# Softmax sums and V products on 32-column tiles of the matmul array, and a new order of all steps, in a sliding-window attention and gMLP kernel

## The chip, the cores and the metric

The kernel runs on one core of one Trainium2 chip. Its time is the device time in microseconds (us) of one execution. The engines are PE (TensorE: matmul), ACT (ScalarE), DVE (VectorE), POOL (GpSimd) and SP (SyncE, which issues nearly all DMAs). Matmuls write to PSUM, which holds eight banks of 128 partitions by 512 f32.

## The reference

The inputs are q, k and v of shape [8, 8, 576, 64] (batch, head, position, head dimension) in f32, and the weights of a gMLP block. Per batch:

```
scores = (q @ k.T) / 8, kept where 0 <= t - s < 64, else -1e9
attn   = exp(scores - max); attn /= sum(attn) + 1e-9
x      = (attn @ v) with the heads side by side        # [576, 512]
h      = relu(x @ w_in)                                # [576, 1024]
u, v   = h[:, :512], h[:, 512:]
v_n    = (v - mean(v)) / sqrt(var(v) + 1e-6)           # over the 512
v_s    = w_spatial @ v_n + b_spatial                   # over positions
out    = (u * v_s) @ w_out                             # [576, 512]
```

## The kernel before

The program is a list of named steps. Each step belongs to an engine and has inputs and buffers that it must wait for. A long text, ORDER, gives the order in which steps are issued, with the engine of each and the number of the buffer or PSUM bank that it takes. Each engine works through its own steps in that order, and semaphores make it wait for the steps of other engines. So the order around any step is written out by hand, with no scheduler behind it. In a name such as `P4_10` the first digit is the batch, the next the half g of the heads (four heads each), and the last a part. `_r` stands for the remainder (the last 64 positions), `_0` to `_4` in the gMLP steps for blocks of 128 rows, the fifth being 64 wide.

Attention, per batch and half:

- `ldq`, `ldk`, `ldv` are loads, issued by SP in order, into buffers `nat` (eight, also used for the weights) and `natv` (four). `cq`, `ck`, `cv` cast to f16, `tq`, `tk` transpose q and k on DVE, and `sl`, `su`, `s4` make a copy of v shifted by 64 positions. POOL, ACT and DVE share the casts and copies.
- `S` (line 490, remainder 557): the scores, transposed, in products of 32 rows of the array by 128 columns, four side by side, 64 positions wide. Their result fills two pairs of banks.
- `E` (L497, on ACT) takes the exponential of two heads at a time into `e2`; `M` (L500, on DVE) takes the minimum with a mask, which zeroes what lies outside the window.
- `Z` (L513, remainder 580): the softmax sums, as a product with ones. Two matmuls of 64 columns side by side, one for each of two heads, put each head's sums on 64 partitions. There are two Z steps per half, one for each pair of heads, u = 0 and 1.
- `N` and `n` (L539, L541, both on ACT): logarithm of the sums, then exp of its negative, which is the reciprocal.
- `P` (L524, remainder 593): the product with v, for each 64 positions and two heads, two matmuls of 64 columns side by side. `X` (L532, 601; DVE) multiplies it with the reciprocal and leaves x transposed, two heads (128 rows of x) per tile.

The gMLP block, per batch:

- `V` (value half of x @ w_in), then `Vr` (relu, ACT, L658), `Vb` and `Va` (statistics, DVE, L660, L662), `L1` and `L2` (ACT, L705, L707), `A` (normalize into `vn`, DVE, L717). `V_4` (L691, L694) pairs the last 64 rows of one batch with the last output rows of the batch before and always uses two tiles of 64 columns.
- `U` (the other half) and `Ur` (relu, ACT, L746); `G` (the spatial product) and `Ge` (times u, DVE, L776); `O` (the product with w_out), `Oe` (copy to `ob`, ACT, L635) and `st` (store, SP).

`V`, `U`, `G` and `O` go through the helper `halves`. It issues each product either whole (128 x 128, L608) or as two halves of 64 columns side by side (L611). A rule, `halved`, picks the halved ones from ORDER: those that stand between Z or P steps, which use 64 columns too. `D` steps (L816) are products of zeros that fill time before real work is ready; there are 27, and their place is in ORDER.

Weights are loaded in pieces (`ldwin`, `ldwsp`, `ldwo`) and cast (`cwin`, `cwsp`, `cwo`). `ldwin100` to `ldwin111` bring the value half of w_in, `ldwin000` to `ldwin011` the other. `W` transposes w_spatial on PE and `We` copies it out of PSUM.

## Time and profile before

| | |
|---|---|
| median of 3 runs | 199.65 us (199.64 to 199.70) |
| span of the profiled execution | 198.2 us |
| mean granted PE clock | 0.998 |
| matmuls, all instructions | 3337, 7839 |
| DMA traffic, mean rate | 42.74 MB, 216 GB/s |
| L513 (Z), 64 matmuls of 64 columns by 512 | 386 ns each, overlapping |
| L524 (P), 512 matmuls of 64 columns by 64 | 196 ns each, overlapping |
| L497 (E), 32 on ACT | 1024 ns |
| L316 (casts of q and k), 10 on ACT | 1156 ns |
| L319 (the same on POOL), three pieces each | 530 and 559 ns a piece |
| L431 (transposes), 32 on DVE | 1246 and 1240 ns |

The profiled execution's span stands 1.4 us below the median of the runs: a run's time also holds what lies around the first and last instruction. The busy time of an engine is the union of its instructions; matmuls overlap in the array, so the time that a PE step costs is read from the starts of successive steps in the timeline, not from the duration of one matmul. The idle time shown for an engine counts only where that engine is the one that others wait for.

### The profile page before, as it was taken

How to read it: one execution, taken by the hardware profiler on the slowest of the kernel's cores; microseconds unless marked ns; L12 is line 12 of the kernel's file. 1: busy time of each engine (PE TensorE's matmuls, PEld its weight loads, DVE VectorE, ACT ScalarE, POOL GpSimd, SP SyncE). 2: the span in 40 equal slices, each digit the busy share in tenths (PEclk: the TensorE clock that was granted, in tenths of full speed). 3: DMA queues.
4: the chain of work that ended last, by engine and by line, in shares of the span. 5: the costliest groups of instructions: out<-in, count | busy, mean ns of one | idle time of the engine just before them, and what ended most of it. 6: DMA issues, size and time to landing. Idle time of an engine off the chain costs nothing.

```text
span 198.2 us, 7839 instructions
## 1 busy us (share of the span) xinstructions
PE 187.3 (94%) x3337; PEld 109.7 (55%) x3337; DVE 158.4 (80%) x306; ACT 168.4 (85%) x305; POOL 76.9 (39%) x147
## 2 busy tenths in 40 slices
PE   7788999999999999989999999999999999999991
PEld 2333565666556665565476567466465565764450
DVE  4799999999796899869999798887958684757420
ACT  2589889878899999989999999999999999558341
POOL 5232584747776689121999299100000000000000
PEclk9999999999999999999999999999999999999999
DMA  6998999999689989989999993878721110500535
GB/s 221 384 289 178 383 365 222 308 366 372 140 203 286 343 239 255 276 195 266 322 253 235 262 294 83 251 205 228 235 107 65 49 41 5 215 0 0 179 115 187
DMA packets 50278, 42.74 MB, mean 216 GB/s; under 512 B 39361, under 2 KB 39489, under 8 KB 50242
## 3 DMA queue, kind: packets, MB, share of 16 engines
q1 hardware_dynamic: 50018, 41.91, 71.9%
q8 instruction: 26, 0.43, 0.9%
q10 hardware_dynamic: 224, 0.33, 0.5%
q14 instruction: 10, 0.08, 0.1%
HBM read 32.79 MB, written 9.44 MB: 213 GB/s over the span
## 4 chain that ended last, share of the span: by engine, by line
PE 42%; ACT 20%; DMA 20%; DVE 6%; SPq 5%; issue 3%; POOL 3%; POOLq 0%
PE bank L611 17%; PE bank L608 17%; DMA nv<-in_v_dram 9%; DMA nk<-in_k_dram 7%; SPq L445 4%; DMA ws<-in_moe_w_spatial_dram 4%; ACT e L497 3%; ACT ob L635 3%; ACT lz L539 3%; ACT hs L316 2%; ACT lz L541 2%; PE pair L490 2%; PE bank L524 2%; ACT ru L746 2%; ACT vs L658 2%
## 5 line engine op out<-in xcount | busy, mean ns | idle before, releaser
L497 ACT ACTIVATE e<-pair 128x1024 f16<-128x1024 f32 x32 | 31.8, 1024 | 2.8 <-PE pair L490 2.6
L611 PE MATMUL bank<-wspT,vn 128*64 128x512 f16 (+3 forms) x440 | 32.4, 296 | 0.3
L776 DVE TENSOR_TENSOR g<-bank,ru 128x512 f16<-128x512 f32 (+1 forms) x40 | 24.6, 629 | 9.1 <-PE bank L608 4.4
L660 DVE BATCH_NORM_STATS2 st<-vs 128x6 f32<-128x512 f16 (+1 forms) x40 | 25.7, 671 | 2.8 <-ACT vs L658 2.8
L658 ACT ACTIVATE vs<-bank 128x512 f16<-128x512 f32 (+1 forms) x40 | 23.0, 602 | 5.6 <-PE bank L611 3.2
L532 DVE TENSOR_TENSOR x<-bank,lz 128x512 f16<-128x512 f32 x32 | 21.4, 683 | 6.5 <-PE bank L524 5.0
L746 ACT ACTIVATE ru<-bank 128x512 f32<-128x512 f32 (+1 forms) x40 | 21.6, 562 | 4.5 <-PE bank L608 4.4
L635 ACT COPY ob<-bank 128x512 f32<-128x512 f32 (+1 forms) x39 | 22.8, 589 | 2.1 <-PE bank L608 1.9
L611 PEld LDWEIGHTS <-vn 128*64 128x64 f16 (+1 forms) x440 | 18.6, 110 | 10.7 <-issue 1.3
L319 POOL CAST hk<-nk 128x384 f16<-128x384 f32 x33 | 16.3, 530 | 19.3 <-DMA nk<-in_k_dram 18.9
L500 DVE TENSOR_TENSOR e<-e,mask 128x1024 f16<-128x1024 f16 x32 | 21.9, 701 | 1.2 <-ACT e L497 1.2
L611 PE MATMUL bank<-win,x 128*64 128x512 f16 x184 | 22.4, 379 | 0.0
L431 DVE STREAM_TRANSPOSE qT<-hq 128x576 f32<-128x576 f32 x16 | 19.8, 1240 | 3.2 <-POOL hq L319 3.0
L611 PE MATMUL bank<-x,win 128*64 128x512 f16 (+1 forms) x288 | 22.3, 298 | 0.0
L431 DVE STREAM_TRANSPOSE kT<-hk 128x576 f32<-128x576 f32 x16 | 19.9, 1246 | 0.7 <-POOL hk L319 0.4
L541 ACT ACTIVATE lz<-lz 128x512 f32<-128x512 f32 x32 | 19.7, 635 | 0.1
L539 ACT ACTIVATE lz<-bank 128x512 f32<-128x512 f32 x32 | 18.6, 606 | 1.2 <-PE bank L513 1.1
L717 DVE TENSOR_SCALAR vn<-vs,mv,ln 128x512 f16<-128x512 f16 (+1 forms) x40 | 15.8, 447 | 4.2 <-ACT ln L707 4.1
L319 POOL CAST hq<-nq 128x384 f16<-128x384 f32 x30 | 15.7, 559 | 7.4 <-DMA nq<-in_q_dram 6.4
L322 POOL COPY hs<-hv 64x512 f16<-64x512 f16 (+1 forms) x28 | 16.2, 607 | 4.4 <-issue 3.7
L816 PE MATMUL bank<-scratch 128*128 128x512 f16 (+1 forms) x68 | 15.6, 379 | 1.3 <-DVE scratch L257 1.3
L611 PE MATMUL bank<-wout,g 128*64 128x512 f16 x128 | 16.1, 380 | 0.0
(89 smaller groups left out, 333.0 us busy)
## 6 DMA issues: line engine op xcount, KB each, us to landing
nq<-in_q_dram SPq DMA_DIRECT2D x16, 576.0 KB, 6.0
nk<-in_k_dram SPq DMA_DIRECT2D x16, 576.0 KB, 5.8
nv<-in_v_dram SPq DMA_DIRECT2D x64, 128.0 KB, 5.2
out_dram<-ob SPq DMA_DIRECT2D x14, 512.0 KB, 4.7
wi<-in_moe_w_in_dram SPq DMA_DIRECT2D x8, 256.0 KB, 6.0
ws<-in_moe_w_spatial_dram SPq DMA_DIRECT2D x4, 288.0 KB, 7.0
nv<-in_v_dram SPq DMA_DIRECT2D x16, 64.0 KB, 4.8
wo<-in_moe_w_out_dram SPq DMA_DIRECT2D x4, 256.0 KB, 8.1
```

Source lines behind the costliest of these rows:

```text
L319: nc.gpsimd.tensor_copy(o[:, n:n + 384], i[:, n:n + 384])
L431: d = add(f"t{name}{b}_{g}", ("DVE", 1.09), key, lambda e: nc.vector.transpose(qt.t[:, :].rearrange("p (i j) -> p j i", j=18), h.t[:, :].b ...
L497: ex = add(f"E{b}_{g}{u}", ("ACT", 0.91), key, lambda e, u=u: nc.scalar.activation(e2[u].t[:, :, :], sc[u].t[:, :, :], AF.Exp, bias=0.0, s ...
L539: a = add(f"N{tag}", ("ACT", 0.06 + 0.00083 * n), key, lambda e: nc.scalar.activation(lz.t[:, 0:n], zb.t[:, 0:n], AF.Ln), deps=[z], acq=[l ...
L541: c = add(f"n{tag}", ("ACT", 0.09 + 0.00083 * n), key, lambda e: nc.scalar.activation(lz.t[:, 0:n], lz.t[:, 0:n], AF.Exp, bias=0.0, scale= ...
L608: nc.tensor.matmul(o[:, :], w, x, start=start, stop=stop)
L611: nc.tensor.matmul(o[c:c + 64, :], w[:, c:c + 64], x, start=start, stop=stop)
L635: lambda e: (nc.vector.tensor_copy if last else nc.scalar.copy)(view(), m.t[rows, 0:n]),
L658: rl = add(f"Vr{b}_{j}", ("ACT", 0.49), key, lambda e: nc.scalar.activation(vs.t[0:jn, :], m.t[0:jn, :], AF.Relu), deps=[pv], acq=[vs], us ...
L660: s1 = add(f"Vb{b}_{j}", ("DVE", 0.6), key + 0.02, lambda e: nc.vector.bn_stats(st6.t[0:jn, 0:6], vs.t[0:jn, :]), deps=[rl], acq=[st6], us ...
L746: lambda e, m=m, ru=ru, n=n: nc.scalar.activation(ru.t[:, 0:n], m.t[:, 0:n], AF.Relu), deps=[pu], acq=[ru], uses=[m])))
L776: lambda e, m=m, g=g, ru=ru, n=n: nc.vector.tensor_tensor(g.t[:, 0:n], m.t[:, 0:n], ru.t[:, 0:n], ALU.mult),
```

## The change

Three things change in the products, and ORDER is new from the first word to the last.

Z becomes one step per half: four matmuls of 32 columns, side by side, one for each head, so each head's sums stand on 32 partitions. There is one N and one n per half in place of two. P keeps two steps per half, but each now covers all four heads and every second head dimension: f = 0 the even, f = 1 the odd ones. It is made of 32-column matmuls, 32 in a step in place of 16, and reads v with a stride of 2. So a tile of x holds the even or the odd dimensions of four heads, and the rows of w_in are loaded in that order (even rows in one tile, odd rows in the other, 2 KB per row as before). The remainder's Z, N and n are 128 wide in place of 256, and `X_r` reads the reciprocal twice by a broadcast.

```diff
-        for u in (0, 1):
...
-                    for w in (0, 1):
-                        nc.tensor.matmul(zb.t[64 * w:64 * w + 64, :], ones[:, :], e2[u].t[:, w, :],
-                                         start=True, stop=True)
...
+                for hh in range(4):
+                    nc.tensor.matmul(zb.t[32 * hh:32 * hh + 32, :], ones[:, 0:32],
+                                     e2[hh // 2].t[:, hh % 2, :], start=True, stop=True)
+        z = add(f"Z{b}_{g}", ("PE", 0.22), key + 0.03, emit_Z, deps=mins, acq=[zb], uses=e2, mode="q")
...
-                        for w in (0, 1):
-                            nc.tensor.matmul(ob.t[64 * w:64 * w + 64, 64 * c:64 * c + 64],
-                                             vv[:, c // 2, 2 * u + w, :],
-                                             e2[u].t[:, w, 64 * c:64 * c + 64],
+                        for hh in range(4):
+                            nc.tensor.matmul(ob.t[32 * hh:32 * hh + 32, 64 * c:64 * c + 64],
+                                             vv[:, c // 2, hh, f:64:2],
+                                             e2[hh // 2].t[:, hh % 2, 64 * c:64 * c + 64],
                                              start=True, stop=True)
```

The gMLP products are whole or in four quarters of 32 columns; none is halved any more. Which are in quarters is written in ORDER (engine `PQ` in place of `PE`): 74 steps.

```diff
-HALVED = halved(2) | {f"U0_{i}" for i in range(5)}
+QUARTERED = {w.split(":")[0] for w in ORDER.split() if w.split(":")[1] == "PQ"}
...
     def halves(name, o, w, x, start, stop):
-        if name not in HALVED:
-            nc.tensor.matmul(o[:, :], w, x, start=start, stop=stop)
-            return
-        for c in (0, 64):
-            nc.tensor.matmul(o[c:c + 64, :], w[:, c:c + 64], x, start=start, stop=stop)
+        n = 32 if name in QUARTERED else 128
+        for c in range(0, 128, n):
+            nc.tensor.matmul(o[c:c + n, :], w[:, c:c + n], x, start=start, stop=stop)
```

```diff
-                                 st.t[:, 512 * f:512 * f + 512], moe_w_in[256 * g + 128 * f:256 * g + 128 * f + 128, cs]),
+                                 st.t[:, 512 * f:512 * f + 512],
+                                 moe_w_in[256 * g:256 * g + 256, cs].rearrange(
+                                     "(p f) n -> f p n", f=2)[f]),
```

The new order also hands casts and copies to other engines:

| step | before | after |
|---|---|---|
| cq | POOL 10, ACT 5, DVE 1 | POOL 11, ACT 4, DVE 1 |
| ck | POOL 11, ACT 5 | POOL 11, ACT 3, DVE 2 |
| cv | POOL 12, DVE 5, ACT 3 | POOL 16, ACT 3, DVE 1 |
| sl | ACT 10, POOL 7, DVE 3 | POOL 11, DVE 6, ACT 3 |
| su | POOL 13, DVE 4, ACT 3 | POOL 14, DVE 4, ACT 2 |
| s4 | POOL 8, ACT 7, DVE 1 | POOL 12, ACT 4 |

Four places of the new ORDER that matter below, cut from it. The first is the start of SP's loads, with the casts and PE steps between:

```diff
+ldq1_0:DQ:6 ... ldk1_1:DQ:7 ... ldq1_1:DQ:0 ... ldwin100:DQ:1 ... ldv1_10:DQ:2 ... ldwin101:DQ
...
+X1_00:DVE:3 ... tk2_0:DVE:3 S2_0:PE:0:1
+X1_01:DVE X1_11:DVE V1_1:PE:2
...
+s45_1:POOL ... ldv7_10:DQ:2 ... ldq6_0:DQ:1 ... cq6_0:POOL:3 ... sl5_00:POOL:3 ... s45_0:POOL ... ck7_0:POOL:0 ... su5_00:POOL
+P5_00:PE:3
...
+O7_2:PE:1 Oe7_2:ACT:1 st7_2:DQ
+U7_4:PE:0 O7_3:PE:2 Ur7_4:ACT:2 Ge7_4:DVE:9 O7_4:PE:1
```

Of the fillers, 23 now stand ahead of `V0_2`; `D12` stands just before `U0_1`, and `D11`, `D18` and `D8` stand in batches 1, 4 and 7.

## The prediction

> **What bounds the kernel now.** I read the page's busy shares first, then the stretches, the PE groups by shape, and the timeline.

> ```profile
> PE 187.3 (94%) x3337; PEld 109.7 (55%) x3337; DVE 158.4 (80%) x306; ACT 168.4 (85%) x305; POOL 76.9 (39%) x147
> ```

> ```profile
> core 0: us, PE busy (x) PEld busy (x) DVE busy (x) ACT busy (x) POOL busy (x), PEclk, DMA share, GB/s
> ...
> 45.00:70.00 25.00, 24.52 (x512) 15.72 (x496) 21.97 (x41) 23.52 (x44) 17.24 (x32) 1.00 0.94 268
> 70.00:95.00 25.00, 23.87 (x517) 14.28 (x513) 22.68 (x44) 23.68 (x43) 12.71 (x25) 1.00 0.93 246
> 95.00:120.00 25.00, 25.00 (x482) 14.96 (x482) 23.64 (x40) 24.27 (x47) 20.40 (x39) 1.00 0.93 267
> 120.00:145.00 25.00, 24.93 (x395) 14.27 (x392) 20.70 (x44) 24.81 (x47) 4.57 (x10) 1.00 0.67 194
> 145.00:170.00 25.00, 24.92 (x495) 15.05 (x493) 17.36 (x34) 24.68 (x45) 0.00 (x0) 1.00 0.17 58
> ```

> PE is full and ACT is nearly as full: 23.5 to 24.8 of every 25 us. DVE is close behind until 120 us. So there are two near-limits, PE and ACT, and a third, DVE, in the first 120 us. The chain of waits agrees, and two groups of ACT show what the change takes from it:

> ```profile
> PE 42%; ACT 20%; DMA 20%; DVE 6%; SPq 5%; issue 3%; POOL 3%; POOLq 0%
> ```

> ```profile
> L541 ACT ACTIVATE lz<-lz 128x512 f32<-128x512 f32 x32 | 19.7, 635 | 0.1
> ...
> L539 ACT ACTIVATE lz<-bank 128x512 f32<-128x512 f32 x32 | 18.6, 606 | 1.2 <-PE bank L513 1.1
> ```

> The numbers behind the bar are the group's busy us, then the mean ns of one. PE leads the chain, ACT and the loads share the rest.

> A busy PE is not a PE at its peak, so I price its work by start times in the timeline:

> ```profile
> 101.73 0.41 PE L513 MATMUL bank<-e,ones 128*64 128x512 f16 x2
> 101.95 0.25 PE L524 MATMUL bank<-e,hv 128*64 128x64 f16 x4
> ...
> 103.06 0.30 PE L580 MATMUL bank<-er,ones 128*64 128x128 f16 x4
> 103.17 1.05 PE L611 MATMUL bank<-wout,g 128*64 128x512 f16 x8
> 104.04 0.25 PE L524 MATMUL bank<-e,hv 128*64 128x64 f16 x4
> ```

> ```profile
> 143.75 1.25 PE L608 MATMUL bank<-wspT,vn 128*128 128x512 f16 x5
> 144.84 0.63 PE L608 MATMUL bank<-x,win 128*128 128x64 f16 x16
> 145.40 0.68 PE L490 MATMUL pair<-qT,kT 32*128 32x64 f16 x64
> 146.01 0.30 PE L580 MATMUL bank<-er,ones 128*64 128x128 f16 x4
> ```

> Five full products take 144.84 - 143.75 = 1.09 us, 217 ns each (216 by finer starts). Eight half ones take 104.04 - 103.17 = 0.87 us: a pair, two 64-column matmuls side by side, costs the same 217 ns. A Z step (one pair) takes 0.22 us, Z_r (two pairs of 128) 0.11 us. Sixteen P matmuls take 0.25 us by their starts: 15.6 ns each, 31 ns per pair. S runs four matmuls on 32 rows each side by side: 64 take 0.61 us, 7.8 ns each or 31 ns per four, plus a gap. That gap is the price of changing shape: the first start after a full product of another shape comes 312 ns after the last one, not 216, so 96 ns, and the same for every change of shape in the trace.

> **Where PE loses time.** I sum PE's steps in listed order at these prices, fillers (D) left out: 166 us stand ahead of the last product, O7_4, which starts at 193.46. So 27.4 us are lost ahead of it: 20.3 by 30.2 us (U0_2, 9.9 us of work done: loads and start-up), 25.4 by 88.6 us, 27.4 at the end. What the change can win beyond PE's own work is in the 7 us after the start-up, 5 of them between 30 and 89 us.

> **The change, part by part.**

> *Z.* Sixteen (batch, half) groups had two Z steps of one pair each and get one step of four quarter matmuls. If a quarter pack (four matmuls of 32 columns) costs the 216 ns that a full product and a pair cost, 16 x 0.216 = 3.46 us go; Z_r saves one 55 ns pack in eight batches, 0.44. All of it is on PE.

> *P.* Twice the matmuls, half the columns: 288 packs before and after. At 31 ns per pack, the S row for four side by side, the cost is 0. At 15.6 ns per matmul, the P row, a pack is 62 ns. I take 31: S shows matmuls, each with its own weight load, starting 7.8 ns apart. The stride of 2 in the weights is also in S's kT reads.

> *74 gMLP steps in quarters.* 297 packs of 512 and 92 of 64; before, 356 and 164 were pairs. At 216 and 31 ns the cost is 0; fewer 64-wide packs in pieces saves 0.15. The trace has no product with four full-height streams. Lower bound 0, because one and two streams both take 216. Upper bound two pairs in a row, 432 ns: 313 packs (with Z) x 0.216 = 68 us. I take 0, since neither one to two streams nor S's four tiles cost anything, and keep 1 ns per pack = 0.31 us for the range. Weight loads become four per pack; one of 64 columns shows 110 ns, one of 128 shows 98, and they run beside the 216 ns of the pack ahead (PEld is 55% busy).

> *Shape changes.* Counting both listings: 48 become 63 between real steps, because V_4 stays in pairs and more products run whole: +15 x 0.096 = +1.44 us.

> PE's own work: -3.46 - 0.44 - 0.15 + 1.44 = **-2.6 us**.

> *ACT.* Sixteen N (606 ns) and sixteen n (635 ns) go: -19.9 us. The remainder's pair shrinks from 256 to 128 elements, by the slope of these rows 8 x 0.215 = -1.7. Casts and copies move to POOL (two ck, one cq, seven sl, three s4 and others): about -10. ACT falls from 168 to some 137 us, POOL rises to about 90, DVE stays at 158 (its X and M count is unchanged; X_r reads its factor broadcast, 421 ns before and between that and the 683 of a 512-wide X now: 0 to 2.1 us over eight, DVE's idle 40 us cover it). ACT stops being a limit. But PE lost only 2 us after 89 us although ACT was 97 to 99% busy there; the 5 us before that come with DVE at 88 to 95% too. I give back 2.4 of the 7 us.

> *Start-up.* In SP's queue the last value half of w_in now stands behind all eight q/k loads of two batches and one piece of batch 1's v. By bytes, 1.28 MB more lie ahead of it, 3.4 us at the page's best 384 GB/s; but SP stood blocked twice in the old order (v issues of 3.19 and 2.47 us), which may shrink. For the u half (before U0) it is 0.77 MB, 2.0 us. V0_1 needs that half; it started at 23.6 with 4.5 us of work done and now has 4.0 ahead of it. Bounds 0 to 2 us; I take 0.8, as V0_1 to V0_2 cover 5.5 us of waiting for the u half. Batch 2's loads are wanted earlier (S2_0 after 15.5 us of work, was 23.0): tk2_0 stands ahead of X1_01 and X1_11 on DVE, and V1_1 waits for these: +0.8. Four fillers (0.43 each) stand later, after D12; a filler in a gap costs nothing, else +1.3 for three; D25 and D26 (1.0) go from the same phase. Net 0.

> *SP's queue later.* ldq6_0 now stands behind ldv7_10, which waits until s45_1 on POOL frees its buffer; that place is 1.2 us of PE work ahead of cq6_0, where it was 7.7. Behind cq6_0 on POOL stand sl5_00, s45_0, ck7_0 and su5_00, for which P5_00 waits. POOL's buffers are free long before, so it can run ahead: 0 to 3.4 us, I take 0.2. Stores ahead of a reused ob buffer can issue 4 us or more before; nothing.

> *Tail.* U7_4 moves behind O7_2, so Ur7_4 (0.38) and Ge7_4 (0.42) with their hand-overs, about 1.05 us, lie beside O7_3 alone (0.86): +0.2.

> Sum: -2.6 - 2.4 + 0.8 + 0.8 + 0.2 + 0.2 = -3.0, and some of the reordering's waits may share one gap, -0.2. So -3.2 on a span of 198.2 (the median lies 1.4 above it): **196.4 us**.

> **Rivals.**

> *The floor is per matmul.* If a column-tiled matmul cannot start sooner than P's 15.6 ns, the 380 packs of 64 (288 + 92) take 62 instead of 31 ns: +11.8 us, **208.2**. For it: the P row itself. Against it: S at 7.8 ns. It decides from 39 ns a pack (380 x 8.4 ns = 3.2 us). [...]

> *Four streams are slower than two.* From 10 ns a pack (313 x 10 ns) the gain is gone; at 288 ns, as if only three ran at once, +22.5 us, **219**. For it: no row shows four. Against: two cost nothing. [...] The trace shows the two of a Z pair starting 4 ns apart, yet the next pair 216 ns after the first, so the offset is not added.

> *DVE takes the place of ACT.* Between 60 and 84 us of PE work the new listing gives DVE 28.5 us of row durations (27.5 with their overlap) against 24.0 of PE. If DVE arrives there without a lead, +3.5: **199.9**, no gain. For it: DVE's 22 to 23.6 of 25 us now. Against: the stretch ahead gives it 9.9 for 12. It decides when more than 3 us are lost there.

> *ACT was the cause of nearly all waits.* Then 4.5 more than PE's work goes: **192.5**.

> **How the numbers follow.** Forecast 0.58; ACT the cause 0.08; waits come back on DVE or in SP's queue 0.17, of which 0.07 within 0.2% (0.4 us, about what a measurement of this kernel can tell from no change) and 0.10 slower; streams slower by 10 ns or more 0.10; floor per matmul 0.07. Faster 0.66, same 0.07, slower 0.27. The range runs from 192.5, the ACT case, to 201.0, which takes in the returned waits and the slow start-up (2.0 for 0.8, 3.4 for 0.2 in SP's queue) and leaves out the floor, most of the streams case and half of the ACT case, 0.2. The forecast's own range is 193.2 to 199.

> **What would show it.** Right: Z steps of 0.22 us from start to start, P steps of 0.25, quarter products 0.86 (V, U, O) and 1.08 (G); ACT near 137 us, POOL near 90; V0_1 near 24.5 us, about 164 us of PE work and some 26.5 us lost ahead of O7_4. Wrong: a P step of 0.5 us (floor); quarter products above 0.90 (streams); PE waiting for DVE tiles x or vn between 80 and 110 us; SP issuing q loads of batch 6 less than 6 us before S6_0.

## The result, and the profile after

The changed kernel takes **223.1 us** (220.7 to 226.6, four runs) against 199.6 for the kernel before, measured beside it: a ratio of 1.115, 95% interval 1.108 to 1.123. The prediction said 196.4, range 192.5 to 201.0, and put 0.27 on slower. It was wrong in sign and outside its range. Its slowest rival, four streams at 219 us, comes near in time, but the traces show another mechanism. Medians count all runs; ratios and intervals, here and below, leave out runs over 1.5% above the fastest of their kernel, among them one of a_vlong at 307.8 us with a granted clock of 0.56.

The profiled execution took 220.7 us with a span of 218.9. From its page (busy shares, then the granted clock and DMA share in 40 slices, then the queue that brings instructions, then the chain of waits):

```profile
PE 191.4 (87%) x4560; PEld 103.3 (47%) x4560; DVE 164.5 (75%) x304; ACT 143.6 (66%) x260; POOL 92.6 (42%) x174
...
PEclk9999799967999999959999999999999999999999
DMA  6999999998999799980588806878005103221423
...
q8 instruction: 35, 0.57, 1.1%
...
PE 74%; DVE 8%; DMA 7%; issue 7%; SPq 1%; ACT 0%; DVEq 0%
```

ACT is relieved, by 25 of the 31 us forecast, and PE leads the chain alone. But PE's busy share falls to 87%, its clock dips three times, and 7% of the chain is "issue": time in which PE waited for nothing that the profile shows. This one has 35 packets on the instruction queue; the kernel before had 26:

```profile
q8 instruction: 26, 0.43, 0.9%
```

The groups of ACT that shrank are as priced, half as many at the same duration:

```profile
L518 ACT ACTIVATE lz<-lz 128x512 f32<-128x512 f32 x16 | 10.1, 630 | 0.2
L516 ACT ACTIVATE lz<-bank 128x512 f32<-128x512 f32 x16 | 9.5, 596 | 3.7 <-PE bank L489 3.5
```

The timeline of the changed kernel, where PE runs without a gap, shows the prices of the new shapes:

```profile
99.88 1.06 PE L588 MATMUL bank<-wout,g 128*32 128x512 f16 x16
100.75 1.05 PE L588 MATMUL bank<-win,x 128*32 128x512 f16 x16
101.62 0.24 PE L557 MATMUL bank<-er,ones 128*32 128x128 f16 x4
```

Sixteen quarter matmuls of 512 take 101.62 - 100.75 = 0.87 us, so a pack of four costs 217 ns like one full product. P's packs of four start 29 ns apart in the median and 32 in the mean, gaps left out (priced at 31); Z steps take 0.22 us. Every price of the prediction's PE sum holds. The windows and the waits of PE show where the time is lost instead (columns: us, busy time and count for each engine, clock, DMA share, GB/s):

```profile
25.00:45.00 20.00, 14.97 (x384) 7.38 (x384) 16.56 (x26) 14.49 (x25) 12.05 (x22) 1.00 1.06 297
45.00:70.00 25.00, 24.16 (x497) 12.89 (x500) 21.45 (x40) 18.42 (x34) 18.96 (x33) 0.86 1.03 271
70.00:95.00 25.00, 19.84 (x588) 10.72 (x575) 18.66 (x31) 15.73 (x29) 14.98 (x29) 0.96 1.00 272
95.00:120.00 25.00, 25.00 (x571) 13.42 (x564) 21.83 (x45) 19.50 (x36) 11.96 (x23) 0.91 0.58 162
120.00:145.00 25.00, 21.75 (x686) 13.18 (x685) 21.33 (x35) 18.07 (x32) 12.96 (x24) 1.00 0.60 171
```

```profile
PE bank L501 <- issue: 9.2, 6, 3.0
PE pair L467 <- DVE kT L408: 2.4, 1, 2.4
PE bank L588 <- issue: 2.2, 2, 1.2
...
PE pair L467 <- ACT hs L291: 1.5, 1, 1.5
PE pair L467 <- issue: 1.2, 1, 1.2
```

PE works 5.2 us less than the window from 70 to 95 us and 3.3 us less from 120 to 145, where 1.1 and 0.1 us were missing before, and its longest waits end on "issue", most of them inside P steps (L501). One such place in the timeline:

```profile
42.46 0.20 PE L501 MATMUL bank<-e,hv 128*32 128x64 f16 x3
45.67 0.21 PE L501 MATMUL bank<-e,hv 128*32 128x64 f16 x1 [3.01 <-issue]
...
46.89 3.59 PE L588 MATMUL bank<-win,x 128*128 128x512 f16 x8
50.28 1.49 PE L588 MATMUL bank<-x,win 128*128 128x512 f16 x3
```

The gap falls between the third and the fourth matmul of one pack, which wait for nothing different. And after it, eight full products take 3.4 us to the next start, at 50.28: 424 ns each in place of 216. PE ran at half clock; the trace's clock record shows 0.5 from 44.97 to 51.80 us, and also from 21.08 to 24.49 and from 92.76 to 99.59 us.

**What the gaps have in common.** Numbered in order of issue from 0, the matmul behind every gap of this kind is number 95 + 128k. Between the gaps that end at 25.85 and 45.67 us lie exactly the 384 = 3 x 128 matmuls of the first window above. The page counts 4560 weight loads for 4560 matmuls, so 128 matmuls are 256 instructions; 4560 pairs are 35.6 such blocks, and the queue q8 brought 35 packets (0.57 MB, 16 KB each; 26 for the 3337 pairs of the kernel before). In all nine gaps over 0.6 us PE goes on 1.37 to 1.61 us after the end of a q8 packet: the packet ahead of 45.67 ran from 43.12 to 44.20. I read this as PE running out of instructions. The kernel before shows one such gap (0.94 us, 1.59 us after a packet), at matmul 94 + 128k, one place off:

```profile
87.89 0.51 PE L490 MATMUL pair<-qT,kT 32*128 32x64 f16 x43 [0.75 <-issue]
```

The trace also shows how far ahead the blocks are brought. In the changed kernel exactly one q8 packet starts between the first matmul of each block and that of the next, for all 34 pairs, and at a gap it is the packet that PE waits for. So in this trace the next block is not asked for, or at least not moved, before PE has begun the one ahead of it. Where the data loads keep the DMA engines under a tenth busy in the first microsecond of a block (nine blocks), the packet starts 0.3 to 1.5 us into it, 0.8 in the median; where over nine tenths (sixteen blocks), 1.2 to 4.4 us, 2.3 in the median. The packet itself takes 1.0 and 1.1 us. With the 1.4 us from its end to the first use, a block that causes no gap has to last an estimated 3.2 us in a quiet stretch and 4.8 us among loads, by these medians; 128 P matmuls at 7.8 ns last 1.0 us.

By the packets just counted, PE here has the block that it works on and at most one more. And the ends of the blocks cost time: with 7.8 ns from matmul to matmul in P, ten of them cost 13.2 us.

I split the start of the last product, O7_4, by the prediction's method: PE's steps at their prices, then the gaps at block ends (less 0.2 us each, an ordinary step from start to start), then what 512- and 256-wide products take beyond their price (half clock), then the rest, which are waits for other engines and the start.

| us | before | changed | difference |
|---|---|---|---|
| PE's work ahead of O7_4 | 166.9 | 164.3 | -2.6 |
| gaps at block ends | 0.7 | 13.2 | +12.5 |
| half clock | 0.4 | 4.5 | +4.1 |
| other waits | 25.5 | 31.4 | +5.9 |
| start of O7_4 | 193.5 | 213.4 | +19.9 |
| behind it, to the span's end | 4.7 | 5.5 | +0.8 |

(The prediction put 166 and 27.4 for the kernel before; here the shape changes beside fillers count too. The split is that of one profile of each kernel, and the terms are not independent: a gap can cover a wait that would else have shown.)

### The profile page after: what moved, and what is told of

It is laid out like the page before. It is cut to its first block, busy times and chain, and to the rows that moved or that the text cites. A ratio compares the mean times of both kernels' runs of the same rounds, so it can differ in the third digit from the quotient of the medians.

```text
span 218.9 us, 10284 instructions
## 1 busy us (share of the span) xinstructions
PE 191.4 (87%) x4560; PEld 103.3 (47%) x4560; DVE 164.5 (75%) x304; ACT 143.6 (66%) x260; POOL 92.6 (42%) x174
## 4 chain that ended last, share of the span: by engine, by line
PE 74%; DVE 8%; DMA 7%; issue 7%; SPq 1%; ACT 0%; DVEq 0%
PE bank L588 57%; PE bank L501 4%; PE pair L467 4%; DMA nk<-in_k_dram 3%; PE bank L668 3%; DMA nv<-in_v_dram 3%; DVE e L477 2%; DVE hs L299 2%; PE bank L489 2%; PE bank L793 1%; DVE st L637 1%; DVE x L509 1%; DMA out_dram<-ob 1%; DVE qT L408 1%; PE bank L368 1%
## 5 line engine op out<-in xcount | busy, mean ns | idle before, releaser
L588 PE MATMUL bank<-wspT,vn 128*32 128x512 f16 (+5 forms) x815 | 44.2, 302 | 0.0
L588 PE MATMUL bank<-x,win 128*32 128x512 f16 (+3 forms) x556 | 39.8, 313 | 1.2 <-issue 1.2
L588 PE MATMUL bank<-wout,g 128*32 128x512 f16 (+1 forms) x344 | 34.1, 403 | 1.0 <-issue 1.0
L588 PE MATMUL bank<-win,x 128*32 128x512 f16 (+1 forms) x284 | 33.5, 387 | 0.0
L635 ACT ACTIVATE vs<-bank 128x512 f16<-128x512 f32 (+1 forms) x40 | 23.6, 597 | 12.3 <-PE bank L588 9.7
L588 PEld LDWEIGHTS <-vn 128*32 128x32 f16 (+2 forms) x815 | 22.4, 96 | 17.1 <-issue 0.6
L297 POOL COPY hs<-hv 64x512 f16<-64x512 f16 (+1 forms) x46 | 26.5, 603 | 4.3 <-ACT hv L291 3.1
L477 DVE TENSOR_TENSOR e<-e,mask 128x1024 f16<-128x1024 f16 x32 | 25.1, 795 | 1.7 <-ACT e L474 1.5
L588 PEld LDWEIGHTS <-win 128*32 128x32 f16 (+1 forms) x556 | 18.3, 98 | 16.4 <-issue 4.7
L408 DVE STREAM_TRANSPOSE kT<-hk 128x576 f32<-128x576 f32 x16 | 19.9, 1246 | 0.7 <-ACT hk L291 0.7
L408 DVE STREAM_TRANSPOSE qT<-hq 128x576 f32<-128x576 f32 x16 | 19.9, 1241 | 0.1
L588 PEld LDWEIGHTS <-g 128*32 128x32 f16 (+1 forms) x344 | 13.1, 100 | 13.2 <-issue 3.1
L588 PEld LDWEIGHTS <-x 128*32 128x32 f16 (+1 forms) x284 | 12.7, 98 | 13.5 <-issue 2.5
```

Source lines behind the costliest of these rows:

```text
L297: nc.gpsimd.tensor_copy(o[:, lo:hi, :, :], i[:, lo:hi, :, :])
L408: d = add(f"t{name}{b}_{g}", ("DVE", 1.09), key, lambda e: nc.vector.transpose(qt.t[:, :].rearrange("p (i j) -> p j i", j=18), h.t[:, :].b ...
L477: mins.append(add(f"M{b}_{g}{u}", ("DVE", 0.65), key, lambda e, u=u: nc.vector.tensor_tensor(e2[u].t[:, :, :], e2[u].t[:, :, :], mask[:, : ...
L588: nc.tensor.matmul(o[c:c + n, :], w[:, c:c + n], x, start=start, stop=stop)
L635: rl = add(f"Vr{b}_{j}", ("ACT", 0.49), key, lambda e: nc.scalar.activation(vs.t[0:jn, :], m.t[0:jn, :], AF.Relu), deps=[pv], acq=[vs], us ...
```

## The experiments

Theory 1: PE's instructions arrive too slowly for the bursts of short matmuls, while the loads fill the DMA engines. Theory 2: the new order of the steps makes PE wait. Theory 3: matmuls of 32 columns are slow in themselves. Times are medians; the kernel before took 198.9 to 200.5 beside them. "Gaps", "half" and "other" are the terms of the table above, from the profiled execution, whose gaps fall a little differently each time.

| label | matmuls | time | ratio to before, interval | PE work | gaps | half | other |
|---|---|---|---|---|---|---|---|
| before | 3337 | 199.6 | | 166.9 | 0.7 | 0.4 | 25.5 |
| changed | 4560 | 223.1 | 1.115 (1.108-1.123) | 164.3 | 13.2 | 4.5 | 31.4 |
| a_whole | 3393 | 215.6 | 1.079 (1.071-1.087) | 169.0 | 9.7 | 3.4 | 28.9 |
| a_pq5 | 3870 | 215.4 | 1.082 (1.077-1.087) | 168.2 | 9.0 | 3.1 | 28.7 |
| b_quart | 5117 | 232.4 | 1.157 (1.149-1.165) | 166.4 | 26.0 | 5.4 | 29.6 |
| b_split | 4237 | 207.8 | 1.045 (1.040-1.049) | 167.9 | 5.6 | 2.9 | 25.9 |
| a_vlong | 4560 | 215.2 | 1.081 (1.075-1.087) | 164.3 | 12.0 | 3.2 | 27.2 |
| b_vlong | 3337 | 200.9 | 1.010 (1.007-1.014) | 166.9 | 2.0 | 0.4 | 25.8 |
| a_late0 | 4560 | 223.0 | 1.109 (1.101-1.118) | 164.3 | 17.5 | 5.1 | 31.1 |
| a_late | 4560 | 232.6 | 1.166 (1.157-1.174) | 164.3 | 24.3 | 5.6 | 33.7 |
| a_p128 | 4048 | 215.4 | 1.072 (1.065-1.079) | 163.6 | 9.1 | 2.3 | 32.4 |
| a_wp128 | 2881 | 206.9 | 1.030 (1.024-1.037) | 168.2 | 0.8 | 1.0 | 31.4 |
| b_p128 | 3081 | 198.8 | 0.997 (0.995-1.000) | 166.1 | 0.0 | 0.6 | 25.5 |
| a_start | 4560 | 221.5 | 1.111 (1.106-1.116) | 164.3 | 13.8 | 4.3 | 33.0 |
| a_old128 | 2881 | 209.0 | 1.046 (1.042-1.050) | 168.6 | 1.7 | 1.4 | 31.1 |
| a_old | 3393 | 216.5 | 1.085 (1.078-1.092) | 169.3 | 4.8 | 3.0 | 33.4 |
| a_old2p | 2881 | 203.6 | 1.017 (1.010-1.024) | 169.0 | 0.4 | 0.4 | 27.9 |
| a_old2 | 3393 | 211.9 | 1.062 (1.054-1.070) | 169.7 | 4.4 | 1.2 | 30.0 |

(In a_old, the 5.9 and 32.3 us that an expectation below quotes count a gap of 1.35 us as a block end; the trace puts it down to a wait for ACT. So with one of 0.85 us in a_p128, a wait for POOL.)

### Is it the quarters, the order, or the number of matmuls?

**a_whole**, the changed kernel with its gMLP products whole, and **a_pq5**, with quarters from batch 5 on only:

```diff
-QUARTERED = {w.split(":")[0] for w in ORDER.split() if w.split(":")[1] == "PQ"}
+QUARTERED = set()                                        # a_whole
+QUARTERED = {w.split(":")[0] for w in ORDER.split()
+             if w.split(":")[1] == "PQ" and int(w[1]) >= 5}   # a_pq5
```

> The changed kernel in its own order, but with all 74 quartered gMLP steps issued whole: 3393 matmuls for 4560. Shape changes rise from 79 to 129, PE's work by 4.6 us. Theory 1 (instruction supply: PE gets its instructions in blocks of 256, 128 matmuls with their weight loads; a block that lasts less than its fetch takes leaves PE idle, and after more than 3 us of idleness PE's clock is halved for a while): the block-end stalls fall from 15.4 to under 5 us, the 5 us at half clock go, so 202 to 211 us. Theory 2 (the new order itself, its loads and DVE waits, costs the time): nothing is won back and the shape changes come on top, 224 to 228 us. Theory 3 (32-column tiles are slow): Z and P keep them, so part of it stays, 210 to 220 us.

> The changed kernel with quarters only from batch 5 on, where the queue of loads is short; whole products before: 3870 matmuls, PE work +3.9 us. Theory 1: the stalls of the first 120 us fall as in the whole variant, few come late, 201 to 210 us and within 3 us of the whole variant. Theory 2: 223 to 227 us. Theory 3: between the whole variant and the changed kernel by the share of quartered steps left.

Measured 215.6 and 215.4, 8 us faster than the changed kernel and alike, but some 5 us above theory 1's ranges: I had taken the gaps to fall under 5 us with the quarters, and 9 to 10 us of them stay, in the bursts of S and P. The time of a_whole also lies in theory 3's range. For the 3 us of idleness in its theory 1 the changed kernel's trace has two gaps, of 3.20 and 3.14 us, inside which half clock begins; as a threshold it is an estimate from these two, and a_late and a_late0 do not bear it out (last section). The 477 quarter matmuls that a_pq5 has over a_whole, all in batches 5 to 7, cost nothing that can be told. The next two decide.

**b_quart**, the kernel before, in its old order, with each matmul of 64 columns issued as two of 32 (Z, Z_r, P, P_r, the halved gMLP products, V_4 and O_4):

```diff
-        for c in (0, 64):
-            nc.tensor.matmul(o[c:c + 64, :], w[:, c:c + 64], x, start=start, stop=stop)
+        for c in (0, 32, 64, 96):
+            nc.tensor.matmul(o[c:c + 32, :], w[:, c:c + 32], x, start=start, stop=stop)
```

> The kernel before in its own order, with the same steps, waits and loads, but every product of 64 columns (Z, P, the halved gMLP steps, V_4, O_4) issued as 32-column matmuls: 5118 matmuls for 3337; the sums are not merged, ACT's work stays, shape changes stay at 63. Theory 1: 40 blocks for 26, block-end stalls of 10 to 30 us, so 212 to 235 us. Theory 2 (order): the order is the old one, so 199 to 202 us. Theory 3: slower by the packs, seen in the starts (a quarter pack over 230 ns, P packs over 35 ns) and not at block ends.

**b_split**, the kernel before with its 512-wide gMLP products issued as two of 256 columns of the moving side. The tiles keep their shape (128 or 64 columns) and PE's work its length; only the number of instructions grows:

```diff
+    COLS = (slice(0, 256), slice(256, 512))
...
+        for n in COLS:
-            halves(f"O{b}_{j}", m.t, ...)
+            halves(f"O{b}_{j}", m.t[:, n], ...)
```

> The kernel before, with each 512-wide whole or halved gMLP product issued as two of 256: 4237 matmuls, no 32-column tile anywhere, array time up by some 2.5 ns per extra start, 544 packs, 1.4 us. Theory 1: 33 blocks for 26; the added instructions lie in long products, where a block still lasts over 5 us, so some stalls at block ends: 201 to 210 us. Theories 2 and 3: 200.5 to 201.5 us, with no gap at block ends beyond the one of 0.9 us at 88 us that the kernel before has.

Both came out as theory 1 says: 232.4 and 207.8. The order is the old one in both, so theory 2 does not make these losses; b_split has no tile of 32 columns, so theory 3 doesn't make its loss either, and in b_quart theory 3's sign is missing: quarter packs of 512 start 216 ns apart in the median and P's packs 30 ns, not over 230 and 35. For b_split's estimate of 2.5 ns per extra start the trace of the kernel before has products of 512 columns 216 ns apart and the pairs of 256 in O7_4 109 to 110: two of these take 2 to 4 ns more. The longest waits of PE, of b_quart and then of b_split, end on "issue":

```profile
PE bank L525 <- issue: 9.7, 6, 3.5
PE bank L615 <- issue: 8.3, 8, 2.0
```

```profile
PE bank L580 <- issue: 2.6, 1, 2.6
PE bank L524 <- issue: 2.4, 1, 2.4
```

### Why do the blocks come late?

**a_vlong** and **b_vlong**: the changed kernel and the kernel before with v loaded in long rows.

```diff
-  nv.t[0:sn, c, :, :],
-  v[b, 4 * g:4 * g + 4, 128 * c:128 * c + sn, :].transpose([1, 0, 2])
+  nv.t[0:sn, c, :, :].rearrange("p h d -> p (h d)"),
+  v[b, 4 * g:4 * g + 4, :, :].rearrange("h (i j) d -> (h i) (j d)", j=4)[128 * c:128 * c + sn, :]
```

> The changed kernel with v loaded in rows of 1 KB in place of pieces of 256 bytes: the same bytes in a quarter of the pieces, from the wrong rows of v. Two readings of why PE's instruction blocks come late. 1a: a block waits behind the loads in the DMA engines; with shorter loads the stalls at block ends (13.2 us in the changed kernel's profile) fall to under 9 us, and the time from 223 to 212-219. 1b: a block takes its time whatever else is in flight; the stalls stay at 12-15 us and the time at 220-226. Rival (the new order is the cause): 220-226 too, with the gaps where they were.

> Control: the kernel before with the same long rows of v. It has one stall of 0.9 us, so the loads can change little by way of the instructions: 196-200 by every reading. What it gains below 199.5 is the worth of the faster loads by themselves, to be taken off the gain of the changed kernel.

The time of a_vlong, 215.2, lies in 1a's range, but its gaps are 12.0 us and not under 9; what fell most is "other", from 31.4 to 27.2; of that, P's wait for the shifted v fell from 1.8 to 0.6 us, the rest was not traced. And the control did not gain: at 200.9 it lies outside its range and lost 1.9 us, 1.3 of it in gaps (one of 2.2 us at 26.5 us). So this pair does not tell 1a from 1b. It suggests that the changed kernel leans harder on its loads than the kernel before.

**a_late** adds loads where there were few; **a_late0** is its control with 16 columns in place of 1152:

```diff
+    for i in range(18):
+        st = buf("nat", f"xx{i}")
+        add(f"xx{i}", ("ACT", 0.45), 6.0, lambda e, st=st, i=i: nc.scalar.dma_start(
+            st.t[:, :], q[i % 8, 0:4, :, :].rearrange("h (i j) d -> (h i) (j d)", j=18)), acq=[st], ...)
```

> Control for the extra loads: the same 18 issues on ACT's queue, each of 16 columns (8 KB). By every reading 222-226: the issues cost ACT some 18 x 0.06 us and the DMA engines next to nothing, and no block end after 160 us gets a new gap.

> The changed kernel and 18 extra loads of 576 KB each, of data that nobody reads, issued from ACT's queue in batches 5 and 6 (about 160 to 195 us), where the DMA engines move little and no block end stalls but one of 0.65 us. 1a (a block waits behind the loads): new gaps at the block ends after 160 us, 4-12 us together, and 226-236. 1b (fixed time for a block): no new gaps, within 1.5 us of the control.

223.0 and 232.6: +9.6 us for loads whose data nobody reads. No run shows the 0.06 us per issue of a_late0's expectation; with its 18 issues the control took 223.0, without them the changed kernel 223.1. By the table, gaps take 6.8 us of the difference, other waits 2.6 and half clock 0.5. From 170 to 195 us, the control first and then a_late:

```profile
170.00:195.00 25.00, 24.32 (x724) 13.96 (x725) 17.31 (x37) 16.75 (x36) 0.00 (x0) 1.00 0.33 99
```

```profile
170.00:195.00 25.00, 16.99 (x496) 9.60 (x492) 10.26 (x22) 10.92 (x22) 0.00 (x0) 0.98 0.76 257
```

With the DMA share at 0.76 in place of 0.33, PE issues 496 matmuls in place of 724. Not all of that is instructions: 2.7 us, up to 194.90, are a wait for a copy on ACT, which itself waited 3.6 us for a store of `out`. Behind 160 us a_late has gaps of 1.6, 3.1, 0.5, 1.4 and 3.1 us at block ends, the control of 1.0 and 0.4. One of them:

```profile
175.01 0.62 PE L466 MATMUL bank<-wout,g 128*32 128x512 f16 x8
178.38 0.61 PE L466 MATMUL bank<-wout,g 128*32 128x512 f16 x8 [2.75 <-issue]
```

Its packet ran from 176.05 to 177.18, late but hardly longer than others (about 1.0 us): it started 3.9 us behind the first matmul of the block ahead, where the control's packet for the same block started 1.1 us behind. So 1a holds: the block waits to start while data fills the DMA engines. A fixed time for a block (1b) does not fit. Where on its way the packet is held up the traces do not show.

### Does the number of matmuls in P's bursts make them?

**a_wp128** (gMLP whole), **a_p128** (with quarters) and the control **b_p128**: P in 128-wide pieces. The work of PE stays the same within 0.8 us; there are 512 fewer matmuls, 256 in the control.

```diff
-                    for c in range(8):
-                        vv = hv.t if c % 2 == 1 or c == 0 else hs.t
+                    for c in range(4):
                         for hh in range(4):
-                            nc.tensor.matmul(ob.t[32 * hh:32 * hh + 32, 64 * c:64 * c + 64], vv[:, c // 2, hh, f:64:2], ...
+                            nc.tensor.matmul(ob.t[32 * hh:32 * hh + 32, 128 * c:128 * c + 128], hv.t[:, c, hh, f:64:2], ...
```

> The changed kernel with its gMLP products whole (as in a_whole, 215.6) and P in 128-wide pieces: each piece of 64 queries takes the v rows of its neighbour, so the values of V products are other ones, the work of PE is the same within 0.8 us, and 512 matmuls fewer are issued (2881 in place of 3393). Theory 1 (PE runs out of instructions in the bursts of short matmuls): the stalls at block ends, 9.7 us in a_whole, fall to under 3 us, and the time to 201-207. Theory 2 (the new order): 212-216. What is left above the kernel before then is the order's part and that of the shape changes.

> The changed kernel, quarters of the gMLP kept, with P in 128-wide pieces (values as in a_wp128): 4048 matmuls in place of 4560, the work of PE the same within 0.8 us. Theory 1: the stalls at block ends fall from 13 us to 5-10 us, and the time from 223 to 213-219. Theory 2: 221-224.

> Control: the kernel before with P in 128-wide pieces (other values of V products): 3081 matmuls in place of 3337, the work of PE the same within 0.8 us. It has one stall of 0.9 us to lose: 197.5-199.7 by every theory.

All three came out as theory 1 says: 206.9, 215.4 and 198.8. From a_whole to a_wp128 the matmuls fall by 15%, the gaps by 8.9 us and the time by 8.7. But a_wp128 still is 7.6 us above the kernel before with hardly a gap left. Its "other" waits are the changed kernel's, 31.4. So theory 2 keeps a share. The two steps of runs also price the change's own terms: the 74 steps in quarters cost 7.5 us net (223.1 against a_whole's 215.6, which has 4.7 us more work), and the doubling of P's matmuls 8.7 us.

### What is the order's share?

**a_start** moves two steps at the start:

```diff
-... ldb:DQ:4 cq0_1:POOL:2 ldv0_00:DQ:1 ... S0_r:PE:1:0 ldq1_0:DQ:6 ...
+... ldb:DQ:4 cq0_1:POOL:2 ldq1_0:DQ:6 ldv0_00:DQ:1 ... S0_r:PE:1:0 ...
-... tq1_0:DVE:5 S1_0:PE:1:0 X0_00:DVE:0 ... P0_01:PE:3 P0_r:PE:2 ...
+... tq1_0:DVE:5 X0_00:DVE:0 ... P0_01:PE:3 P0_r:PE:2 S1_0:PE:1:0 ...
```

> The changed kernel with two steps moved at its start: the load of batch 1's first q goes ahead of batch 0's v on SP's queue, and S1_0 stands behind the four P steps of batch 0 on PE in place of ahead of them. If the late start (V0_1 at 28.2 us against 23.6) carries through to the end: V0_1 at 24-26 and the time 2-4 us below the changed kernel, 218.5-221. If PE is held to the pace of its instructions while the DMA engines are full, the start is given back at the next block ends: within 1.5 us of 223.

221.5, inconclusive: V0_1 did not come earlier (28.8 us), because P then waited 2.8 us for hs, the shifted v, on POOL, where it had waited 1.8. The late start is not S1_0's place alone.

**a_old128** and **a_old** put the changed kernel's steps into the old order: ORDER of the kernel before, with the two Z, N and n steps of a half replaced by one. gMLP is whole in both, P is 128 wide in a_old128.

> The steps of the changed kernel in the order of the kernel before (each merged Z and N at the place of the later of its two; 17 of 1065 steps stand a little later, where their data or buffer comes later), gMLP products whole, P in 128-wide pieces (values as in a_wp128). It has a_wp128's 2881 matmuls and, within 0.4 us, its work on PE; only the order differs. a_wp128 took 206.85. If the 6 us that a_wp128 still loses in waits are the new order's: 199.5-203 (before 199.2, 1.7 us more work on PE). If they belong to the new Z, P and their reciprocals: 205-208.

> The same with P in its 64-wide quarters: 3393 matmuls, the values of the reference. Against a_whole (215.6, the same instructions in the new order). Instruction supply with the order's part: the bursts of P stall here too, 3-10 us at block ends, and the time is 203-211, over a_old128 by the stalls. If the order alone made the stalls: within 1 us of a_old128.

209.0 and 216.5, outside both readings each time. The trace of a_old128 holds the reason: up to 75.7 us it had lost 24.5 us, like the kernel before (23.0 at 74.6), then 5 us between 76 and 102 us in waits for ACT and DVE. I had merged the steps badly: 17 steps stood later than in the old order. **a_old2p** and **a_old2** put each Z at the first place where its data are there, and no step had to move back:

The parts of batch 3 and 4 around one such place, in a_old and in a_old2 (names only; in the kernel before, X3_10 stood behind M3_11, E4_01 behind X3_00, G2_2 behind E4_00):

```diff
-M3_11 P3_10 O1_3 Z3_1 O1_0 N3_1 P3_00 G2_3 n3_r G2_4 G2_2 n3_0 X3_00 P3_r P3_01 E4_01 E4_00 X3_r S4_1 X3_01 n3_1 X3_10 ...
+M3_11 O1_3 Z3_1 O1_0 N3_1 n3_1 P3_10 X3_10 P3_00 G2_3 X3_00 P3_01 E4_01 G2_4 n3_r X3_01 E4_00 G2_2 P3_r X3_r S4_1 ...
```

> As a_old128 (the changed kernel's steps in the order of the kernel before, gMLP whole, P in 128-wide pieces with other values), but each merged Z stands at the first place where its data are there, N and n follow at the next places, and E5_10, P3_10, P3_01, X3_10 and X3_01 are put where no step has to move back for want of a buffer. a_old128 lost as little as the kernel before up to 75 us (24.5 us against 23.0, 1.7 of it one stall), then 5 us in waits on ACT and DVE between 84 and 93 us, among the steps that had slipped. If those waits came of the slipped steps: the waits apart from stalls and half clock are 25-27.5 us as before, and the time 201.5-205. If the new Z and P bring them in any order: 206.5-209.5.

> The same with P in its 64-wide quarters (3393 matmuls, the reference's values). a_old took 216.5 with 5.9 us of stalls, 3.0 us of half clock and 32.3 us of other waits. If the other waits fall as in a_old2p: 205-212. If not: 214-217.5.

203.6 and 211.9, both times in the range for the order; the other waits of a_old2p, 27.9, lie just above the 25 to 27.5 expected. The same instructions in two orders, a_wp128 and a_old2p, differ by 3.3 us although a_old2p has 0.8 us more work, and by one profile of each 3.5 us of "other" waits go. But their ratios to the kernel before have intervals that just touch (1.024-1.037 and 1.010-1.024), and the second pair, a_whole and a_old2, splits otherwise: 3.7 us apart, with 5.3 us less in gaps and 1.1 us more in other waits in the old order. So the new order costs some 3 to 4 us; whether as waits or through the gaps stays open. The remaining 2.4 us of a_old2p's other waits (27.9 against 25.5) came with the merged Z and P also in the old order; whether a better merge would save them was not tried. The longest waits of a_wp128, then of a_old2p:

```profile
PE bank L587 <- POOL win L299: 3.0, 2, 2.8
PE pair L467 <- DVE kT L408: 1.8, 2, 1.6
```

```profile
PE pair L466 <- DVE kT L407: 2.6, 2, 1.6
PE bank L586 <- DVE x L507: 1.5, 3, 0.9
```

In a_wp128 the new order waits 2.8 us, up to 35.63, for POOL's casts of w_in; a_old2p does not, and neither does the changed kernel's own trace. No run computes the reference and beats the kernel before. Without its quarters, the change spends more than Z and Z_r save (3.9 us) on shape changes: 124 between real steps in a_old2, where the prediction counted 48 before and 63 after, 0.096 us each.

## Why the prediction was wrong, step by step

- **PE's own work, -2.6 us: right.** Z 0.22 us, P some 31 ns per pack, quarter products 217 ns per pack, shape changes 96 ns; 164.3 against "about 164" ahead of O7_4. The rivals "floor per matmul" and "four streams are slower" are refuted by the starts, in the changed kernel and in b_quart (216 and 30 ns). b_quart's loss against the kernel before is 25.3 us in gaps at block ends, 5.0 in half clock and 4.1 in other waits.
- **P and the 74 steps in quarters, cost 0: the step that failed.** The array's price is 0, as said. The prediction asked only whether the array and the weight loads could follow. It did not ask whether PE's instructions could. 1223 more matmuls with their weight loads are nine more packets on q8, and the bursts are denser: +12.5 us of gaps. Taken out one after the other, the quarters were worth 7.5 us and P's extra matmuls 8.7. The profile of the kernel before had both hints: q8's 26 packets, and one "issue" wait of 0.8 us at S4_1.
- **Half clock, not in the sum: +4.1 us.** Two of the three dips begin inside gaps of 3.20 and 3.14 us, and the prediction had no gap of that kind. The first follows the start-up waits and meets only fillers and short products.
- **ACT, 168 to some 137, and POOL some 90: nearly right.** 143.6 and 92.6. DVE, put at 158, rose to 164.5; M alone went from 701 to 795 ns (21.9 to 25.1 us). **Waits given back, -2.4: not seen.** The "other" waits behind 65 us are level with the kernel before, +4.7 and +4.1 us from there to O7_4; ACT's relief brought nothing that can be told.
- **Start-up, +0.8 and +0.8: mis-sized.** V0_1 started at 28.2 us, forecast 24.5. By V1's last step (65 us) "other" stood at 26.7 against 21.4: +5.3 of the +5.9 us. How much of it is the order's is open, as said above. The bound of 2 us came from w_in's bytes in the queue; the trace shows other waits on the way to V0_1: S0_1 1.5 us for ACT (it starts at 12.78 us in place of 12.11), P 1.8 us for the shifted v on POOL, and a first block end (1.24 us). S0_0 waits 2.4 us for kT, but starts when it did before (8.74 and 8.70).
- **DVE takes ACT's place: no.** Between 80 and 110 us PE has no wait above 0.2 us on DVE's x or vn, though the gaps in that stretch may have given DVE time.
- **SP's queue later, +0.2: right** as far as the trace shows: no wait of PE above 0.2 us on a load's cast or transpose behind 60 us.
- **Tail, +0.2: +0.8 behind O7_4.** O7_4 waited some 0.2 us for g, the end of U7_4's path, as priced; but the last store left ACT 1.8 us behind O7_4's start in place of 1.2.

The rival at 219 us was closest for a wrong reason: its sign "quarter products above 0.90 us" did not come (0.87).

## What to carry to other kernels

Cutting products into column tiles cost the array nothing here (217 ns for a pack of four, 216 for a full product), but each cut is an instruction and a weight load that PE has to be brought, here 128 matmuls at a time (35 packets for 4560); count matmuls per microsecond in the dense bursts, and look at what the DMA engines carry there, before calling such a cut free. A gap marked "issue" at matmuls 128 apart, ending 1.37 to 1.61 us after a packet on the instruction queue, was this limit here. Widening the moving side of P took 8.9 us of such gaps away (a_wp128), and cuts in a stretch with few loads cost nothing (a_pq5, 215.4 us against 215.6); spreading the bursts between long products was not tried. And price a start-up from every wait on its chain, not from the bytes of one transfer.
